# Six pairs' plain products ahead of their products of sums, and the first pair by seven products too

## The chip, the cores and the metric

The kernel runs on one core of a Trainium2 chip. Five engines work side by side, each in its own order: TensorE (PE in the profile, its weight loads PEld) for matrix products, VectorE (DVE), ScalarE (ACT) and GpSimd (POOL) for elementwise work, and SyncE (SP), which issues most loads and stores. The metric is the time on the device in microseconds (us), a median over runs. Before the change it is 539.0 us, the median of three runs from 539.0 to 539.04.

## The reference

A gated feed-forward layer over 2048 tokens, in bf16.

```python
B, S, D, F = 1, 2048, 1024, 3584
def _gelu(x):
    return jax.nn.gelu(x, approximate=True)
def reference(x, w_gate, w_up, w_down):
    return (_gelu(x @ w_gate) * (x @ w_up)) @ w_down
```

## The kernel before

**Tiles and halves.** The tokens go in two halves (`h` 0 and 1) of 1024; a half has two blocks of 512 (`tb` 0 and 1). The 3584 columns of gate and up are 28 tiles of 128, two neighbouring tiles make a pair, and a chunk (`chunks[(h, c)]`) is four tiles: 1 MB of gate and 1 MB of up. D = 1024 is eight slices of 128, `kd` 0 to 7; the upper half of the rows is `kd` 0 to 3, the lower half 4 to 7. One matmul takes a 128x128 piece of weights and a 128x512 piece of the transposed x, which is kept as `xT[0]` and `xT[1]`, and adds into one of eight PSUM banks. The banks are used in twos, one for gate (`j` = 0) and one for up (`j` = 1): PB, VB, QB, RB.

**Seven products instead of eight.** For a pair, the two tiles, the two halves of the rows and the two token blocks make a 2x2 by 2x2 block product. `quads` (L406) does it with seven block products of four matmuls, for gate and for up, so 56 matmuls where the plain way takes 64. M1 and M2 (L441 to L452) are plain: the upper and the lower rows of the pair's first tile with `xT[0]`. M5, M6, M7, M3 and M4 are products of sums: `s1` to `s4` and a copy `a22` are made from the weights by `s_sum` (L367), `t1` to `t4` and a copy `b22` from x by `t_sum` (L241). The sums of weights have one buffer each, so those for the next pair (`prep`, L460) are made behind the product that read the old ones: by GpSimd at L388, `a22` by ScalarE at L401. The sums of x are made once in a half, by VectorE at L262 and ScalarE at L251; they are then kept.

In a pair ScalarE copies M1 into Q (L444), M5 into SBUF (L472) and M6 into R (L478), VectorE adds M5 (L434) to Q and to both V, ScalarE applies gelu (L286), and VectorE multiplies gate by up into h (`hT`, L291). M7 and M4 add into R; up's M4 needs the bank from which VectorE has just added M5 into V. Engines that are handed instructions run them in the order in which the code emits them; the helpers `pe`, `dve`, `act`, `pool` and `sp` (L119 to L140) fix that.

**The start.** `first_pair_units` (L329) does pair 0 the plain way: 32 matmuls with `xT[0]` and 32 with `xT[1]` (`part`, L323, `mm_gu`, L265), while the sums of x and those of pair 1 are made. Its first x block is loaded as it lies and transposed on TensorE for `kd` 0 to 3 (`transpose_x0`), the rest comes by transposing DMA (`load_xT`). Loads of the first tiles stand on SyncE's and ScalarE's queues by hand (L187 to L233). Then `quads` runs pair 1 alone, with `thens` entry `early`: the next pair's `s1` and `s2` are made late, a piece of `t4` goes to GpSimd, and `pool_behind_dve` (L136) makes GpSimd wait for VectorE at one place. From pair 2 on `quads` takes two pairs at a time: both M1 and M2, then both pairs' products of sums.

**Work beside it.** In the first half of the tokens VectorE also makes sums of the down weights (`stage_step`, L625), which SyncE stores to DRAM (`t_dram`) for later; there are 42 such steps and four of `s_down`, run a few at a time by `run_steps`. After the 14 pairs `down_group` does h times the down weights, also by seven products, and then the second half follows.

Of the kernel before, what the change touches and what calls it, by code (L numbers as in the profile page):

```python
# [11 lines left out]
F32 = mybir.dt.float32  # L12
# [22 lines left out]
def kernel(  # L35
# [106 lines left out]

    xs0 = w_mem[:, 4 * CH : 4 * CH + TSB * D].rearrange("p (a b) -> p a b", b=D)
    chunks = {}

    def new_chunk(key):
        c0 = 2 * CH * (key[1] % 2)
        chunks[key] = tuple(
            w_mem[:, c0 + j * CH : c0 + (j + 1) * CH].rearrange(
                "p (a b) -> p a b", b=FG  # L150
            )
            for j in range(2)
        )
# [33 lines left out]
    load_x0(0, sp, 0, 2)  # L187
    load_x0(0, act, 2, TSB)
    load_w(first, 0, 0, 2, sp, 0, FA)
    load_x0(1, act)  # L190
    load_w(first, 1, 0, 2, sp, 0, FA)
    load_w(first, 0, 2, 5, act, 0, FA)
    load_w(first, 1, 2, 5, sp, 0, FA)
# [20 lines left out]
    load_xT(xT, 0, 0, KH, KH + 1)  # L214
    behind_transpose = last_on["sp"]
    load_xT(xT, 0, 0, KH + 1, KH + 2)
    for j in range(2):
        load_w(first, j, 5, KD, act, 0, FA)
        tc.add_manual_dep(
            last_on["act"].ins,  # L220
            behind_transpose.ins.name,
            SCHED_DEP,
            reason="engine order",
        )
    act(nc.scalar.preload_act_table(ACT.Gelu_apprx_tanh))
    load_xT(xT, 0, 0, KH + 2, KD)
    for k0, k1 in ((0, 2), (2, KH), (KH, KD)):
        load_xT(xT, 0, 1, k0, k1)
    for j in range(2):
        load_w(first, j, 0, KD, sp, FA, FG)  # L230
    new_chunk((0, 1))
    for j in range(2):
        load_w((0, 1), j, 0, KD)  # L233
# [31 lines left out]
    def mm_gu(ps, w_sb, fi, tb, kd):  # L265
        pe(
            nc.tensor.matmul(  # L267
                ps[:],
                lhsT=w_sb[:, kd, fi * P : (fi + 1) * P],
                rhs=xT[tb][:, kd, :],  # L270
                start=(kd == 0),
                stop=(kd == KD - 1),
            )
        )

# [23 lines left out]
    def unit_out(hT, bset, fi, tb):  # L299
        mult(hT, gelu(banks[bset[0]]), banks[bset[1]], fi, tb)  # L300

    def transpose_x0(q):

        parts = [(2 * q, 0, 4), (2 * q + 1, 0, 4)]
        if q == 0:
            parts = [(0, 0, 2), (0, 2, 4), (1, 0, 4)]
        for n, (kd, ts0, ts1) in enumerate(parts):
            tp = banks[(PB + QB)[(2 * q + n) % 4]][:].bitcast(BF16)
# [14 lines left out]
    def part(held, tb, k0, k1, us=(0, 1), js=(0, 1)):  # L323
        for kd in range(k0, k1):
            for j in js:
                for u in us:
                    mm_gu(banks[held[u][j]], chunks[first][j], u, tb, kd)

    def first_pair_units(hT):  # L329

        held = (VB, RB)
        transpose_x0(0)
        warm(RB[1], TB // 2)
        part(held, 0, 0, KPQ, js=(0,))
        transpose_x0(1)
        part(held, 0, 0, KPQ, js=(1,))
        part(held, 0, KPQ, KD)
        t_sum("t1", 0, KH // 2)
        t_sum("t1", KH // 2, KH)
        for u in range(2):  # L340
            unit_out(hT, held[u], u, 0)
        held = (QB, PB)
        part(held, 1, 0, KH)
        t_sum("t2")
        t_sum("b22")
        t_sum("t3", 0, KH // 2)
        part(held, 1, KH, KD, (0,))
        unit_out(hT, held[0], 0, 1)
        t_sum("t3", KH // 2, KH)
        part(held, 1, KH, KD, (1,))  # L350
        unit_out(hT, held[1], 1, 1)
        for j in range(2):
            s_sum(0, 1, j, "s3", True, False)
        for name in ("s1", "s2", "s4"):
            for j in range(2):
                s_sum(0, 1, j, name)
# [5 lines left out]
    def block(key, j, i, kh):  # L362
        fi = 2 * (key[2] % PPG) + i
        w_sb = chunks[(key[0], key[2] // PPG)][j]
        return w_sb[:, half(kh), fi * P : (fi + 1) * P]
# [40 lines left out]
    def quads(hT, h, members, nxt, thens, m5_first):  # L406

        last = nxt is None
        run = []
        for n, pair in enumerate(members):  # L410
            after = (h, members[n + 1]) if n + 1 < len(members) else nxt
            first_ = (PB, RB)[n] if len(members) > 1 else VB
            run.append((pair, after, thens[n], first_, (QB, VB)[n]))
# [27 lines left out]
        for pair, _, _, first_, q_ in run:  # L441
# [4 lines left out]
        for pair, _, _, first_, _ in run:  # L446
# [8 lines left out]
        for n, (pair, after, then, _, Q_) in enumerate(run):  # L455
            f0 = 2 * pair
            ends = after is None
            eager = "early" in then

            def prep(j, name, after=after):  # L460
                if after is not None:
                    s_sum(after[0], after[1], j, name)
# [6 lines left out]
            def do_m5(j):  # L469
# [3 lines left out]
                if not eager:  # L473
                    prep(j, "s1")
# [6 lines left out]
            if eager:  # L481
# [9 lines left out]
            for j in range(2):  # L491
                add_m5(Q_[j], Q_[j], m5[j])
                if not eager:
                    prep(j, "s2")
            done(n, "m5")
            for j in range(2):
# [4 lines left out]
                if j == 0 and eager:  # L501
                    pool_behind_dve()
                    for name in ("s1", "s2"):
                        for i in range(2):
                            prep(i, name)
# [3 lines left out]
                else:  # L509
                    mult(hT, g, banks[V_[1]], f0 + 1, 1)  # L510
# [9 lines left out]
            for j in range(2):  # L520
# [4 lines left out]
                else:  # L525
                    mult(hT, g, banks[R_[1]], f0 + 1, 0)
# [541 lines left out]
```

## Time and profile before

| what | value |
|---|---|
| median of the runs | 539.0 us |
| the profiled execution, first to last instruction | 537.4 us |
| matmuls (with transposes and warming ones) | 2388 |
| TensorE busy | 533.6 us, 99% |
| VectorE / ScalarE / GpSimd busy | 68% / 49% / 47% |
| chain, pair 0 (L267) | from 4.98 us to 19.82 us, with transposes between |
| chain, pairs 1 to 13 of the first half (L418) | 163.21 us from 19.82 us |
| chain, first half's down product (L698) | 87.89 us from 183.03 us |
| chain, second half's pairs (L418) | 175.56 us from 270.92 us |
| chain, second half's down product (L698) | 87.95 us from 446.48 us |

The profile shows one execution, so its durations add up to its own 537.4 us; the 1.6 us between that and the median lie outside the first and the last instruction. In a line of the timeline the columns are: start (us from the span's start), length (us), engine, line of the kernel, operation, what is written and read, shapes, and how many instructions are merged; a bracket tells how long the engine was idle before it and what ended that.

### The profile page before, as it was taken

Reading aid. Unit: us, or ns where it says so; the run is one execution under the profiler, and the core shown is the slowest. Engines: PE = TensorE matmul, PEld = TensorE weight load, DVE = VectorE, ACT = ScalarE, POOL = GpSimd, SP = SyncE. Lnnn points to the kernel's source line nnn. Section 1 sums busy time; section 2 is a strip of 40 time slices with the busy share of each in tenths; the row PEclk is TensorE's granted clock in tenths of the full one; section 3 lists DMA queues with packets and bytes.
Section 4 is the critical chain, followed back from the end, with each engine's and each line's share of the span. In section 5 each row is a group of like instructions: output and inputs, shape, how many; then the busy total and the mean of one; then the engine's idle time right before and its main releaser. Section 6 shows DMA issues by size and latency. Waiting matters only on the chain.

```text
span 537.4 us, 7033 instructions
## 1 busy us (share of the span) xinstructions
PE 533.6 (99%) x2388; PEld 379.2 (71%) x2388; DVE 367.6 (68%) x476; ACT 263.5 (49%) x447; POOL 252.2 (47%) x213
## 2 busy tenths in 40 slices
PE   9999999999999999999999999999999999999997
PEld 4568686867677686777768676776768686866866
DVE  2985868787876998989555353444444669979961
ACT  2555555556465329117465554656555551452280
POOL 0698696969696200000056494958677670000000
PEclk9999999999999999999999999999999999999999
DMA  9965759697623887788950413314040329677846
GB/s 220 329 199 134 267 164 304 182 320 199 229 53 143 318 288 243 243 292 292 329 168 12 145 62 97 110 48 154 3 156 22 136 84 337 228 237 250 292 143 212
DMA packets 92547, 102.70 MB, mean 191 GB/s; under 512 B 18656, under 2 KB 67424, under 8 KB 92512
## 3 DMA queue, kind: packets, MB, share of 16 engines
q1 hardware_dynamic: 69568, 80.23, 45.7%
q10 hardware_dynamic: 22944, 22.02, 13.2%
q8 instruction: 19, 0.31, 0.3%
q14 instruction: 16, 0.13, 0.1%
HBM read 85.98 MB, written 12.58 MB: 183 GB/s over the span
## 4 chain that ended last, share of the span: by engine, by line
PE 99%; ACT 0%; issue 0%
PE bank L418 63%; PE bank L698 33%; PE bank L267 3%; PE bank L202 1%; PE bank L311 0%; ACT o_sb L754 0%
## 5 line engine op out<-in xcount | busy, mean ns | idle before, releaser
L418 PE MATMUL bank<-t_mem,s_mem 128*128 128x512 f32 x1056 | 244.6, 392 | 0.0
L418 PEld LDWEIGHTS bank<-t_mem,s_mem 128*128 128x128 f32 x1056 | 198.1, 188 | 42.7 <-issue 0.2
L388 POOL TENSOR_TENSOR s_mem<-w_mem 128x512 fp32r<-128x512 bf16 x102 | 124.0, 1236 | 185.5 <-DMA out_dram<-o_sb 96.9
L698 PE MATMUL bank<-t_mem,s_mem 128*128 128x512 f32 (+1 forms) x548 | 127.2, 391 | 0.0
L698 PEld LDWEIGHTS bank<-t_mem,s_mem 128*128 128x128 f32 x548 | 102.5, 188 | 22.0
L291 DVE TENSOR_TENSOR hT<-w_mem,bank 128x512 bf16<-128x512 f32 x106 | 72.5, 687 | 66.5 <-PE bank L418 44.5
L434 DVE TENSOR_TENSOR bank<-bank,m 128x512 f32<-128x512 f32 x108 | 70.0, 694 | 56.1 <-ACT m L472 54.3
L418 PE MATMUL bank<-xT,w_mem 128*128 128x512 bf16 x432 | 95.7, 379 | 0.0
L286 ACT ACTIVATE w_mem<-bank 128x512 f32<-128x512 f32 x106 | 63.0, 597 | 64.1 <-DVE bank L434 34.8
L418 PEld LDWEIGHTS <-w_mem 128*128 128x128 bf16 x432 | 41.2, 98 | 51.3 <-issue 3.4
L388 POOL TENSOR_TENSOR s_mem<-w_mem,s_mem 128x512 fp32r<-128x512 bf16 x52 | 68.4, 1335 | 2.9 <-PE bank L418 2.9
L600 DVE TENSOR_TENSOR t_mem<-w_mem 128x1024 fp32r<-128x1024 bf16 x56 | 65.9, 1225 | 0.9 <-PE bank L418 0.9
L388 POOL TENSOR_TENSOR s_mem<-s_mem,w_mem 128x512 fp32r<-128x512 f32 x52 | 61.3, 1200 | 0.0
L401 ACT CAST s_mem<-w_mem 128x512 fp32r<-128x512 bf16 x54 | 33.2, 616 | 31.3 <-PE bank L418 30.1
L478 ACT COPY bank<-bank 128x512 f32<-128x512 f32 x54 | 30.8, 570 | 26.6 <-PE bank L418 26.6
L670 DVE TENSOR_TENSOR s_mem<-hT 128x512 fp32r<-128x512 bf16 x52 | 36.7, 745 | 7.1 <-PE bank L698 7.1
L472 ACT COPY m<-bank 128x512 f32<-128x512 f32 x54 | 31.8, 589 | 18.4 <-PE bank L418 18.4
L698 PEld LDWEIGHTS <-hT 128*128 128x128 bf16 x224 | 21.3, 98 | 26.6 <-issue 2.1
L444 ACT COPY bank<-bank 128x512 f32<-128x512 f32 x54 | 30.7, 570 | 14.3 <-PE bank L418 13.5
L625 DVE TENSOR_TENSOR o_sb<-wd_sb,o_sb 128x512 fp32r<-128x512 bf16 x28 | 32.9, 1176 | 0.5
L763 ACT CAST o_sb<-bank 128x512 bf16<-128x512 f32 x27 | 14.8, 585 | 33.8 <-PE bank L698 33.8
L597 ACT CAST t_mem<-w_mem 128x1024 fp32r<-128x1024 bf16 x28 | 26.9, 1047 | 0.0
(46 smaller groups left out, 236.5 us busy)
## 6 DMA issues: line engine op xcount, KB each, us to landing
t_mem<-t_dram SPq DMA_DIRECT2D x56, 512.0 KB, 5.3
w_mem<-in_w_gate_dram ACTq DMA_DIRECT2D x10, 1024.0 KB, 5.4
w_mem<-in_w_up_dram ACTq DMA_DIRECT2D x10, 1024.0 KB, 8.3
wd_sb<-in_w_down_dram SPq DMA_DIRECT2D x28, 256.0 KB, 5.4
t_dram<-o_sb SPq DMA_DIRECT2D x28, 256.0 KB, 3.5
wd_sb<-in_w_down_dram SPq DMA_DIRECT2D x12, 512.0 KB, 7.6
w_mem<-in_w_down_dram SPq DMA_DIRECT2D x4, 1024.0 KB, 6.7
w_mem<-in_w_down_dram SPq DMA_DIRECT2D x8, 512.0 KB, 8.3
```

Source lines behind the costliest of these rows:

```text
L286: act(nc.scalar.activation(out=g_sb, in_=ps[:], func=ACT.Gelu_apprx_tanh))
L291: nc.vector.tensor_tensor(out=hT[:, fc, tb * TB : (tb + 1) * TB], in0=g_sb, in1=ps[:], op=ALU.mult,)
L388: pool(nc.gpsimd.tensor_tensor(out=t, in0=in0, in1=in1, op=op))
L401: act(nc.scalar.copy(out=t, in_=a(1, 1)))
L418: nc.tensor.matmul(banks[bank][:], lhsT=lhs[:, c, :], rhs=rhs[:, c, :], start=start and c == 0, stop=c == KH - 1, skip_group_check=True,)
L434: nc.vector.tensor_tensor(out=banks[dst][:], in0=banks[src][:], in1=m5[:], op=ALU.add)
L472: act(nc.scalar.copy(out=m5[j][:], in_=banks[V_[j]][:]))
L478: act(nc.scalar.copy(out=banks[R_[j]][:], in_=banks[Q_[j]][:]))
L600: dve(nc.vector.tensor_tensor(out=t, in0=in0, in1=in1, op=ALU.subtract))
L625: dve(nc.vector.tensor_tensor(out=t, in0=in0, in1=in1, op=ALU.subtract))
L670: dve(nc.vector.tensor_tensor(out=t, in0=in0, in1=in1, op=op))
L698: nc.tensor.matmul(banks[bank][:, c0:c1], lhsT=lhs(i, u), rhs=rhs(i)[:, c0:c1], start=start and i == 0, stop=stop and i == NS - 1, skip_gr ...
```

## The change

For the first half of the tokens, pairs 0 to 5 are formed anew: pair 0 is tiles 4 and 6, pair 1 tiles 5 and 7, pairs 2 to 5 tiles 0 to 3 with 8 to 11 (`LEAD`). Their first tiles, 0 to 5, are done the plain way with `xT[0]` at the very start, two by two (`PLAIN`): the upper rows of tiles 0 to 3, then their lower rows, then tiles 4 and 5. After the upper rows a bank holds exactly M1 of a pair; ScalarE copies it into a part of h's memory that isn't written yet (`hold`), and the lower rows add M2 on top, which gives that tile's first output. Then `quads` runs the six pairs with `plain=False`: no M1 and M2, M1 is fetched back into Q by ScalarE (`fetch`), and only the products of sums are left. So pair 0 too is done by seven products, and there is no `early` order and no `pool_behind_dve` any more; the order of a pair with `plain=False` is M5, M5, M6, M6, and gate's `s3` of the next pair is made by VectorE, the other sums by GpSimd. Chunks (0,1) and (0,3) lie in h's memory. From pair 6 on all is as before, but the staging steps are shared out anew: two in each of pairs 1 to 5, nine in each later two pairs.

The loads at the start are also set anew: gate weights on SyncE, up weights on ScalarE, all four tiles of chunk (0,0) early, then the second x block, chunk (0,1) in halves, and chunk (0,2).

```diff
+    LEAD = ((4, 6), (5, 7), (0, 8), (1, 9), (2, 10), (3, 11))
+    PLAIN = ((0, 1), (2, 3), (4, 5))
+    HF = 16
+    HELD = ((0, 1), (0, 3))
...
+    def p_hold(pair, j):
+        f = ((8, 9), (10, 11), (12, 13), (14, 15), (24, 25), (26, 27))[pair][j]
+        return hT0[:, f : f + 1, :].rearrange("p a b -> p (a b)").bitcast(F32)
...
+    for j, queue in enumerate((sp, act)):
+        ts = slice(j * TSB // 2, (j + 1) * TSB // 2)
+        load_x0(0, queue, ts.start, ts.stop)
+        load_w(first, j, 0, KPQ, queue, 0, FA)
+        load_x0(1, queue, ts.start, ts.stop)
+        load_w(first, j, 0, KPQ, queue, FA, FG)
+        load_w(first, j, KPQ, KH, queue)
...
+    load_xT(xT, 0, 0, KH, KD)
     for j in range(2):
+        load_w(first, j, KH, KD)
+    for k0, k1 in ((0, KH), (KH, KD)):
         load_xT(xT, 0, 1, k0, k1)
+    new_chunk((0, 1))
+    for k0, k1 in ((0, KH), (KH, KD)):
+        for j in range(2):
+            load_w((0, 1), j, k0, k1)
+    new_chunk((0, 2))
     for j in range(2):
+        load_w((0, 2), j, 0, KD)
...
+    def hold(held, tiles, j):
+        for u, t in enumerate(tiles):
+            pair = [top for top, _ in LEAD].index(t)
+            act(nc.scalar.copy(out=p_hold(pair, j), in_=banks[held[u][j]][:]))
...
+        sets = ((VB, RB), (QB, PB), (VB, RB))
+        def top(n, j, k0, k1):
+            plain_products(sets[n], PLAIN[n], j, k0, k1)
+            if k1 == KH:
+                hold(sets[n], PLAIN[n], j)
+        def rest(n):
+            plain_products(sets[n], PLAIN[n], 0, KH, KD)
+            gelus(sets[n], PLAIN[n])
+            plain_products(sets[n], PLAIN[n], 1, KH, KD)
         transpose_x0(0)
         warm(RB[1], TB // 2)
+        top(0, 0, 0, KPQ)
+        top(0, 1, 0, KPQ)
         transpose_x0(1)
+        top(1, 0, 0, KPQ)
+        top(0, 0, KPQ, KH)
+        top(0, 1, KPQ, KH)
+        top(1, 1, 0, KPQ)
+        top(1, 0, KPQ, KH)
+        top(1, 1, KPQ, KH)
+        rest(0)
+        outs(sets[0], PLAIN[0])
         t_sum("t1", 0, KH // 2)
         t_sum("t1", KH // 2, KH)
+        rest(1)
+        outs(sets[1], PLAIN[1])
         t_sum("t2")
+        t_sum("t3", 0, KH // 2)
+        t_sum("t3", KH // 2, KH)
+        top(2, 0, 0, KH)
+        top(2, 1, 0, KH)
         t_sum("b22")
+        rest(2)
+        outs(sets[2], PLAIN[2])
+        for name in ("s3", "s1", "s2", "s4"):
             for j in range(2):
+                s_sum(0, 0, j, name)
...
+        def fetch(n):
+            for j in range(2):
+                act(nc.scalar.copy(out=banks[run[n][4][j]][:], in_=p_hold(n, j)))
...
             def prep(j, name, after=after):
                 if after is not None:
-                    s_sum(after[0], after[1], j, name)
+                    dve_too = not plain and (name, j) == ("s3", 0)
+                    s_sum(after[0], after[1], j, name, dve_too, False)
...
-            if eager:
+            if not plain:
                 order = (do_m5, 0), (do_m5, 1), (do_m6, 0), (do_m6, 1)
...
                 add_m5(V_[j], R_[j], m5[j])
                 if j == 0:
                     done(n, "v of gate")
-                if j == 0 and eager:
-                    pool_behind_dve()
-                    for name in ("s1", "s2"):
-                        for i in range(2):
-                            prep(i, name)
                 prep(j, "s3")
...
+            thens = [{} for _ in LEAD]
+            thens[0]["start"] = [
+                lambda j=j: s_sum(0, 0, j, "a22") for j in range(2)
+            ] + [lambda: t_sum("t4", 0, KH // 2)]
+            thens[0]["m5"] = [lambda: t_sum("t4", KH // 2, KH - 1)]
+            thens[0]["v of gate"] = [lambda: t_sum("t4", KH - 1, KH)]
+            for n in range(1, len(LEAD)):
+                thens[n]["start"] = [lambda: run_steps(1), run_loads]
+                thens[n]["m3"] = [lambda: run_steps(1), run_loads]
...
+            quads(hT, h, range(len(LEAD)), (h, begin), thens, True, False)
...
-                few = lead == begin
-                add(0, "m1", lambda n=3 if few else 4: run_steps(n))
-                add(0, "start", lambda n=1 if few else 3: run_steps(n))
+                add(0, "m1", lambda: run_steps(4))
+                add(0, "start", lambda: run_steps(3))
```

## The prediction

> **What bounds the kernel now.** I read the busy line and the chain first, then TensorE's timeline over the first 60 us, then GpSimd's and VectorE's over the same stretch, then the load rates.
>
> ```profile
> PE 533.6 (99%) x2388; PEld 379.2 (71%) x2388; DVE 367.6 (68%) x476; ACT 263.5 (49%) x447; POOL 252.2 (47%) x213
> ...
> PE 99%; ACT 0%; issue 0%
> ...
> 6.71 13.11 PE L267 MATMUL bank<-xT,w_mem 128*128 128x512 bf16 x60
> 19.66 3.63 PE L418 MATMUL bank<-xT,w_mem 128*128 128x512 bf16 x16
> 22.93 9.52 PE L418 MATMUL bank<-t_mem,s_mem 128*128 128x512 f32 x40
> 32.29 7.08 PE L418 MATMUL bank<-xT,w_mem 128*128 128x512 bf16 x32
> 39.02 18.51 PE L418 MATMUL bank<-t_mem,s_mem 128*128 128x512 f32 x80
> 57.37 2.98 PE L418 MATMUL bank<-xT,w_mem 128*128 128x512 bf16 x13
> ```
>
> The chain is 99% TensorE and each piece begins where the one before ends, so every matmul taken away is a gain and every new wait of TensorE is a loss, one for one. Prices, start to start: a plain product (19.66 - 6.71) / 60 = 0.216 us, a product of sums (57.37 - 39.02) / 80 = 0.229 us, two pairs by seven products 57.37 - 32.29 = 25.08, so 12.54 a pair.
>
> ```profile
> 15.24 2.29 DVE L262 TENSOR_TENSOR t_mem<-xT,t_mem 128x2048 fp32r<-128x2048 bf16 x1
> ...
> 17.32 1.22 POOL L388 TENSOR_TENSOR s_mem<-w_mem 128x512 fp32r<-128x512 bf16 x1 [16.01 <-DMA w_mem<-in_w_gate_dram]
> 17.45 2.18 DVE L262 TENSOR_TENSOR t_mem<-xT 128x1024 fp32r<-128x1024 bf16 x1
> ...
> 20.14 1.58 DVE L262 TENSOR_TENSOR t_mem<-xT 128x1024 fp32r<-128x1024 bf16 x1
> 20.60 3.72 POOL L388 TENSOR_TENSOR s_mem<-s_mem,w_mem 128x512 fp32r<-128x512 f32 x2
> ...
> 44.45 2.31 POOL L388 TENSOR_TENSOR s_mem<-s_mem,w_mem 128x512 fp32r<-128x512 f32 x2
> 46.71 2.74 POOL L388 TENSOR_TENSOR s_mem<-w_mem 128x512 fp32r<-128x512 bf16 x2
> 47.36 1.07 DVE L625 TENSOR_TENSOR o_sb<-wd_sb,o_sb 128x512 fp32r<-128x512 bf16 x1
> ...
> 62.51 0.68 DVE L625 TENSOR_TENSOR o_sb<-wd_sb 128x512 fp32r<-128x512 bf16 x1
> ```
>
> GpSimd's sums and VectorE's sums of two SBUF operands do not run side by side. Two GpSimd sums alone take 2.31 us; with one 512-wide VectorE sum in them 2.74, and that sum takes 1.07 to 1.53 instead of 0.68. The 1024-wide sum at 17.45 begins with a GpSimd sum under way and lasts 2.18. They take turns: a GpSimd sum holds the place for 1.13 (its cadence), a VectorE sum pushes GpSimd back by 2.74 - 2.31 = 0.43 when 512 wide; a 1024-wide one by 0.97 (3.72 - 2 x 1.13 = 1.46, less 0.43 for the 512-wide one also in it). For 2048 wide I take 2.29 - 0.25 = 2.04, the 0.25 being what the narrower ones leave free. VectorE's work on PSUM (L291, L434: 0.64 apart back to back) doesn't compete.
>
> ```profile
> GB/s 0 154 307 315 180 268 278 256 229 196 324 307 322 354 349 354 374 389 261 37 3 0 71 345 372 351 362 402 315 56 11 0 52 216 91 1 0 91 371 368
> ```
>
> This is the rate in slices of 1.5 us over 0 to 60 us.
>
> **The change part by part.** *Fewer matmuls.* Pair 0 goes from 64 plain products (64 x 0.216 = 13.8) to one seven-product pair (12.54): -1.27 us. Nothing else leaves the path; it is the whole gain.
>
> *TensorE's new order, if nothing made it wait.* The first matmul at 4.93 as before, four at the cold pace, four more, eight transposes: 7.57. The other 88 plain products: 7.57 + 88 x 0.216 = 26.56. Marks on the way: the last two tiles' upper rows begin at 19.65, and pair 0's sums run from 26.56 to 26.56 + 40 x 0.229 = 35.74.
>
> *Loads.* Ahead of chunk (0,1) stand both x blocks and chunk (0,0), 4.19 MB; its four halves of 0.52 MB follow. Summing the slices above, 4.22 MB have moved at 18.0 us, 4.70 at 19.5, 5.24 at 21.0, 5.77 at 22.5, 6.32 at 24.0. So the halves land at about 19.6, 21.0, 22.5 and 24.0, against TensorE's 19.65, 21.4, 23.1 and 24.8: just in time, 0 us. Bounds: 18.0 (fewer 512 B packets) and 21.5 (a second stretch of transposes), so 0 to 1.9.
>
> *Pair 0's operands: the step that decides.* Before, six weight sums were ahead on GpSimd, two `s3` on VectorE, and L262's last piece was put on GpSimd behind VectorE by hand (`pool_behind_dve`). Now GpSimd makes all eight of pair 0's, `s3` first though it is wanted last, and at once pair 1's, while VectorE makes `t2`, `t3` and three pieces of `t4`. VectorE is free for `t2` only at 21.15: two multiplications at 16.2, two pieces of `t1` (1.22 each) to 19.93, two multiplications of tiles 2 and 3. Taking turns from 19.8 (end of `t1`):
> s3 20.93; s3 22.1; t2 24.15; s1 25.3; t3 26.25; s1 27.4; t3 28.35; s2 29.5; s2 30.6; t4 31.6 (VectorE multiplies tiles 4 and 5 between t3 and t4).
> M5 of gate starts at 26.56, M5 of up waits for its s1 (27.5), M6 of gate for its s2 (29.55), M6 of up until 30.7 to 31.6, where without waits it ends at 26.56 + 16 x 0.229 = 30.2: +1.4 us.
> Then s4 32.7; s4 33.85. VectorE adds M5 twice (to 33.1), then stands in line with a 512-wide piece of `t4` (34.3), adds M5 to gate's V (35.1), stands again with the last piece of `t4` (behind pair 1's s1: 35.85), and again with pair 1's gate `s3` (behind the other s1: 37.4), and only then adds M5 to up's V: 38.2. Up's M4, four matmuls into that bank, waits for it: 38.2 to 39.15. TensorE would have ended the pair at 35.74, so +3.4 us, the 1.4 included. As one sum: ten GpSimd turns 11.3, VectorE's turns 2.04 + 3 x 0.97 + 3 x 0.43 = 6.2, 19.8 + 17.6 = 37.4, and the add and M4 behind.
> Bounds: if all three narrow VectorE sums find the place free, 33.1 + 3 x 0.68 + 2 x 0.64 = 36.4, M4 ends at 37.3, +1.6; each that has to wait adds 0.6. Upward 4.8, if the weights land 1.4 us late, so that `t2` goes ahead of both `s3` and everything moves. I take 3.4, since GpSimd's next sums have all they wait for and leave no gap.
>
> The Trainium skill (SBUF — State Buffer, section SBUF: two separate sides) says that a VectorE instruction with two SBUF inputs and a GpSimd one exclude each other for the whole instruction. By whole durations the line would be 10 x 1.17 + 2.29 + 3 x 1.22 + 3 x 0.68 = 19.7 instead of 17.6, and the time 543.3, an estimate by that rule; the trace shows 0.43 and not 0.68 for the narrow sum, so I keep the row.
>
> *Pairs 1 to 5*, 9.18 us each without plain products between. GpSimd: 7 x 1.13 + 3 x 0.43 (gate's `s3` and two staging sums on VectorE) = 9.2. VectorE: 7 x 0.64 + 3 x 1.3 = 8.4. After the delay of pair 0, GpSimd is some 2.5 us ahead of need, which covers 5 x 0.02: 0 us; without that lead up to 1. ScalarE's fetch of M1 is not in the trace; by L478 (570 ns) and L401 (616 ns) 1.2 a pair, and its pair comes to 6.6 of 9.18: 0. Copies into h's memory cost L472's 589 ns each beside matmuls: 0.
>
> *Later.* Staging sums move from pairs 1 to 5 into the last two pairs (nine instead of four steps there). At 168.27 VectorE had waited 2.3 us, which takes three sums, and the first down weights leave SP's queue, behind those sums' stores, at about 167.6 instead of 158.76, landing by 176 against a first use at 175.36: 0, at most 0.5.
>
> *Sum against the execution's own time.* Span 537.4 - 1.27 + 3.4 = 539.5. The runs' 539.0 is 1.6 above the span; with that, 541.2.
>
> **Rivals.** *(1) The floor, faster.* If GpSimd's sums are ready when wanted, nothing is late: 539.0 - 1.27 = 537.7. For it: TensorE hid the same contention before, with one wait of 0.2 us at 26.7. Against it: the eighth port turn (`s2` of gate, 29.5) is already past M6's 28.4, even with weights on time. It decides if s2 of up is ready by 29.3 and up's V is added by 34.8.
> *(2) Little more than the first wait.* The narrow sums find gaps, because GpSimd itself waits for TensorE: +1.6, so 539.0 - 1.27 + 1.6 = 539.3. For it: at 30 us before, GpSimd paused 0.7 us for TensorE. Against it: all it needs for pair 1's `s1` is M5 of pair 0, done at 28.4.
> *(3) Weights late.* The gate half of chunk (0,1) comes after 21 and TensorE waits at once, then `t2` goes first: 539.0 - 1.27 + 4.8 = 542.5. For it: the 1 MB loads of this chunk took 10 and 11 us to land before.
>
> **How the numbers follow.** Forecast 55%, (1) 11%, (2) 16%, (3) 18%. 0.2%, what a measurement of this kernel can tell from no change, is 1.08 us: 537.92 to 540.08. The forecast's own bounds are 539.9 (+2.2, one narrow sum waiting) to 542.5 (+4.8). Faster 0.10: nearly all of (1). Same 0.20: (2) and the low edge of the forecast. Slower 0.70: the rest of it and (3). The range takes in (2), down to 539.1, and a little over (3), to 542.8, and leaves out the floor.
>
> **What would show it.** Right: TensorE's plain products end near 26.6; then its first waits, for `s_mem` from GpSimd inside pair 0's M5 and M6 (1 to 2 us), and before the last four matmuls of that pair a wait for VectorE's add (about 2 us); pair 1 starts near 39; 9.2 us a pair from there with no waits; the rest as before, some 2 us later. GpSimd's sums between 20 and 40 us would take 1.6 and more where VectorE has one in between. Wrong: pair 1 starting before 37 (rival 1 or 2), TensorE waiting for a weight load at 19 to 21 (rival 3), or waits in pairs 2 to 5, where I have none.

## The result, and the profile after

The changed kernel takes 545.86 us (median of four runs, 544.74 to 548.17) where the kernel before takes 539.0 (538.65 to 539.04): 1.0131 times as long, 95% interval 1.0107 to 1.0155. It is slower, as forecast, but by 6.9 us and not by 2.2. The profiled execution took 545.35 us, its span 543.1 against 537.4.

Two lines of the profile's page after, as shown of before, and TensorE's timeline from the last two plain tiles to the end of pair 0 (columns as above):

```profile
PE 533.9 (98%) x2380; PEld 380.9 (70%) x2380; DVE 370.1 (68%) x485; ACT 272.4 (50%) x467; POOL 259.6 (48%) x216
...
PE 92%; SPq 2%; POOL 2%; DMA 2%; DVE 1%; ACT 0%; issue 0%; ACTq 0%
```

```profile
22.08 7.08 PE L329 MATMUL bank<-xT,hT 128*128 128x512 bf16 x32 [2.27 <-DMA hT<-in_w_gate_dram]
28.81 3.08 PE L460 MATMUL bank<-t_mem,s_mem 128*128 128x512 f32 x12
32.80 6.03 PE L460 MATMUL bank<-t_mem,s_mem 128*128 128x512 f32 x24 [0.90 <-POOL s_mem L428]
40.50 47.50 PE L460 MATMUL bank<-t_mem,s_mem 128*128 128x512 f32 x204 [1.68 <-DVE bank L476]
```

The chain is no longer 99% TensorE: 8% of it runs over other engines and loads, nearly all ahead of the last line. There are three waits: 2.27 us for the gate half of chunk (0,1) ahead of tiles 4 and 5, 0.90 for GpSimd's `s2` inside M6 (1.24 against the nominal pace, since the piece before it is stretched too), and 1.68 for VectorE's add to up's V ahead of the last four matmuls of pair 0. These four take 4 x 0.229, so pair 1 begins at 41.42; the forecast said 39.15, the pace without waits 35.74.

VectorE's and GpSimd's timelines over the same stretch:

```profile
20.91 2.29 DVE L274 TENSOR_TENSOR t_mem<-xT,t_mem 128x2048 fp32r<-128x2048 bf16 x1
23.11 4.27 DVE L274 TENSOR_TENSOR t_mem<-xT 128x1024 fp32r<-128x1024 bf16 x2
...
30.41 1.32 DVE L274 TENSOR_TENSOR t_mem<-xT,t_mem 128x1024 fp32r<-128x1024 bf16 x1
33.22 0.70 DVE L476 TENSOR_TENSOR bank<-bank,m 128x512 f32<-128x512 f32 x1 [1.50 <-ACT bank L521]
34.63 0.70 DVE L476 TENSOR_TENSOR bank<-bank,m 128x512 f32<-128x512 f32 x1 [0.71 <-ACT bank L521]
35.24 1.45 DVE L274 TENSOR_TENSOR t_mem<-xT,t_mem 128x512 fp32r<-128x512 bf16 x1
36.61 0.69 DVE L476 TENSOR_TENSOR bank<-bank,m 128x512 f32<-128x512 f32 x1
37.21 1.06 DVE L274 TENSOR_TENSOR t_mem<-xT,t_mem 128x512 fp32r<-128x512 bf16 x1
38.19 1.65 DVE L426 TENSOR_TENSOR s_mem<-hT 128x512 fp32r<-128x512 bf16 x1
39.76 0.69 DVE L476 TENSOR_TENSOR bank<-bank,m 128x512 f32<-128x512 f32 x1
```

```profile
22.11 7.40 POOL L428 TENSOR_TENSOR s_mem<-hT 128x512 fp32r<-128x512 bf16 x4 [20.81 <-DMA hT<-in_w_gate_dram]
29.47 3.27 POOL L428 TENSOR_TENSOR s_mem<-s_mem,hT 128x512 fp32r<-128x512 f32 x2
32.71 2.30 POOL L428 TENSOR_TENSOR s_mem<-hT,s_mem 128x512 fp32r<-128x512 bf16 x2
```

The pattern is the one forecast: `t2` (20.91), `t3`, the first half of `t4` on VectorE between GpSimd's eight sums, two of which alone take 2.3 us and four 7.40 with VectorE's in between; then the adds of M5 (L476) with three narrow sums standing between them, the last at 38.19, each 1.06 to 1.65 us long instead of 0.68. All of it is some 2 us later than forecast.

As a sum over the span's +5.7: 1.27 less for the matmuls saved; pair 1 begins 41.42 - 35.74 = 5.68 late; pairs 1 to 5 take 87.84 - 40.50 = 47.34 us where 204 matmuls at 0.229 make 46.7, +0.6; the first down product takes 88.47 from matmul to matmul, 88.05 before, +0.4; some 0.3 is spread. In this execution 2.25 us lie outside its first and last instruction. Before it is 1.8: each of the 47 executions of the kernel before beside the experiments takes 1.74 to 1.85 us more than its own span. The 1.6 given for it above sets the median of the runs against the span of another execution.

One execution among the experiments, the profiled one of plain_c0 (679.5 us), had TensorE's clock at 0.75 from 5.5 us on; only its loads are read below, and that kernel was run again as plain_c0b.

### The profile page after: what moved, and what is told of

Same layout as the page of the kernel before. It is cut to its first block, busy times and chain, and to the rows that moved or that the text cites. A ratio compares the mean times of both kernels' runs of the same rounds, so it can differ in the third digit from the quotient of the medians.

```text
span 543.1 us, 7102 instructions
## 1 busy us (share of the span) xinstructions
PE 533.9 (98%) x2380; PEld 380.9 (70%) x2380; DVE 370.1 (68%) x485; ACT 272.4 (50%) x467; POOL 259.6 (48%) x216
## 4 chain that ended last, share of the span: by engine, by line
PE 92%; SPq 2%; POOL 2%; DMA 2%; DVE 1%; ACT 0%; issue 0%; ACTq 0%
PE bank L460 60%; PE bank L737 32%; POOL s_mem L428 2%; SPq L190 2%; DMA hT<-in_w_gate_dram 1%; DMA w_mem<-in_w_up_dram 1%; DVE t_mem L274 0%; DVE bank L476 0%; DVE s_mem L426 0%; ACT bank L521 0%; SPq L179 0%; ACTq L185 0%; ACT o_sb L793 0%; ACTq L521 0%
## 5 line engine op out<-in xcount | busy, mean ns | idle before, releaser
L460 PE MATMUL bank<-t_mem,s_mem 128*128 128x512 f32 x1096 | 254.4, 392 | 2.7 <-DVE bank L476 1.7
L460 PEld LDWEIGHTS bank<-t_mem,s_mem 128*128 128x128 f32 x1096 | 204.8, 188 | 49.1 <-DVE bank L476 2.0
L428 POOL TENSOR_TENSOR s_mem<-w_mem 128x512 fp32r<-128x512 bf16 x88 | 104.4, 1207 | 155.6 <-DVE t_mem L274 96.3
L737 PEld LDWEIGHTS bank<-t_mem,s_mem 128*128 128x128 f32 x548 | 102.4, 188 | 22.5 <-issue 0.5
L476 DVE TENSOR_TENSOR bank<-bank,m 128x512 f32<-128x512 f32 x112 | 73.2, 694 | 57.7 <-ACT m L516 44.5
L287 ACT ACTIVATE w_mem<-bank 128x512 f32<-128x512 f32 x106 | 62.9, 597 | 60.7 <-DVE bank L476 36.9
L460 PE MATMUL bank<-xT,w_mem 128*128 128x512 bf16 x320 | 70.8, 380 | 0.0
L428 POOL TENSOR_TENSOR s_mem<-w_mem,s_mem 128x512 fp32r<-128x512 bf16 x46 | 61.6, 1361 | 3.4 <-PE bank L460 3.4
L460 PEld LDWEIGHTS <-w_mem 128*128 128x128 bf16 x320 | 30.5, 98 | 38.0 <-issue 2.6
L428 POOL TENSOR_TENSOR s_mem<-s_mem,w_mem 128x512 fp32r<-128x512 f32 x46 | 54.7, 1208 | 0.0
L521 ACT COPY bank<-bank 128x512 f32<-128x512 f32 x56 | 31.9, 571 | 25.7 <-PE bank L460 25.4
L441 ACT CAST s_mem<-w_mem 128x512 fp32r<-128x512 bf16 x48 | 29.6, 616 | 26.8 <-PE bank L460 25.6
L428 POOL TENSOR_TENSOR s_mem<-hT 128x512 fp32r<-128x512 bf16 x14 | 19.8, 1432 | 27.7 <-DMA hT<-in_w_gate_dram 20.8
L486 ACT COPY bank<-bank 128x512 f32<-128x512 f32 x44 | 25.1, 570 | 11.5 <-PE bank L460 10.8
```

The costliest lines, as they stand in the source:

```text
L287: act(nc.scalar.activation(out=g_sb, in_=ps[:], func=ACT.Gelu_apprx_tanh))
L428: pool(nc.gpsimd.tensor_tensor(out=t, in0=in0, in1=in1, op=op))
L441: act(nc.scalar.copy(out=t, in_=a(1, 1)))
L460: nc.tensor.matmul(banks[bank][:], lhsT=lhs[:, c, :], rhs=rhs[:, c, :], start=start and c == 0, stop=c == KH - 1, skip_group_check=True,)
L476: nc.vector.tensor_tensor(out=banks[dst][:], in0=banks[src][:], in1=m5[:], op=ALU.add)
L521: act(nc.scalar.copy(out=banks[R_[j]][:], in_=banks[Q_[j]][:]))
```

## The experiments

What the theories meant by turns: a sum of two SBUF operands on VectorE and one on GpSimd take turns at a shared place. All runs in one table. Pair 0's begin and end are read from TensorE's timeline. Where its first sum is late (after2, v1_free, plain_c0b), it begins when TensorE is through with the plain products. The end is the start of the long run that follows, plus 0.229 for each matmul of it that still belongs to pair 0; the matmul records have it some 0.1 later. In c1_first, v1_free and s3v a stretch at half clock or a short wait lies in those matmuls, so there the end is the start of pair 1's first matmul. The ratios are to the kernel before on the same chip. On the chip of after2, fetch_early and s3v_fetch that kernel took 541.07 us (538.50 to 542.53) and on the others 539.02 to 539.34, so those three are compared by their ratios.

| run | pair 0 begins | ends | takes | median us | ratio, 95% interval |
|---|---|---|---|---|---|
| the change | 28.81 | 41.42 | 12.6 | 545.86 | 1.0131 (1.0107 to 1.0155) |
| after2 | 27.54 | 41.25 | 13.7 | 545.65 | 1.0089 (1.0056 to 1.0122) |
| no_t34 | 28.13 | 38.06 | 9.9 | 542.67 | 1.0061 (1.0043 to 1.0079) |
| c1_first | 26.08 | 44.15 | 18.1 | 548.09 | 1.0188 (1.0148 to 1.0227) |
| s3_last | 28.61 | 40.00 | 11.4 | 543.21 | 1.0073 (1.0058 to 1.0088) |
| v1_free | 28.52 | 42.07 | 13.5 | 544.15 | 1.0094 (1.0078 to 1.0110) |
| plain_c0b | 27.08 | 42.11 | 15.0 | 545.67 | 1.0124 (1.0098 to 1.0150) |
| sums_c0 | 30.55 | 41.58 | 11.0 | 543.04 | 1.0069 (1.0051 to 1.0086) |
| floor | 26.68 | 37.72 | 11.0 | 541.38 | 1.0037 (1.0021 to 1.0053) |
| act_c1 | 28.81 | 41.43 | 12.6 | 544.98 | 1.0102 (1.0061 to 1.0143) |
| s3v | 29.67 | 40.26 | 10.6 | 543.02 | 1.0068 (1.0053 to 1.0083) |
| tidy | 29.75 | 39.77 | 10.0 | 542.90 | 1.0063 (1.0047 to 1.0080) |
| floor_tidy | 27.34 | 38.49 | 11.2 | 541.08 | 1.0033 (1.0020 to 1.0046) |
| fetch_early | 30.79 | 42.55 | 11.8 | 546.65 | 1.0116 (1.0080 to 1.0152) |
| s3v_fetch | 28.80 | 39.29 | 10.5 | 543.89 | 1.0065 (1.0042 to 1.0088) |

**First question: is it the turns, and which of them?**

no_t34:

```diff
+        if name in ("t3", "t4"):
+            tsum[name] = tsum["t2"]
+            return
```

> Leaves out x's sums t3 and t4: their products take t2 in their place. Turns (my theory: pair 0's waits of 3.45 us are VectorE's sums and GpSimd's pushing each other back): five VectorE sums fewer, 3 x 0.97 + 2 x 0.43 = 3.8 us of turns, more than the wait; so pair 0 runs in 9.2 to 9.6 us instead of 12.6, span about 539.8, time about 542. The wait of 2.3 us at the last two plain tiles stays. Rival (GpSimd's eight sums are too long by themselves for the time they have, or the fetch of M1 sets the pace): the waits inside pair 0 stay at 2 us or more, time 544.5 to 546.

Pair 0 takes 9.9 us and no wait for GpSimd or VectorE is left in it, only 0.4 for ScalarE. VectorE's sums cause both waits; 0.3 to 0.7 us more than expected stay.

s3_last:

```diff
-        for name in ("s3", "s1", "s2", "s4"):
+        for name in ("s1", "s2", "s3", "s4"):
```

> Pair 0's sums on GpSimd in the order of their use: s1, s2, s3, s4. Turns: the number of turns is the same, but s2 comes two GpSimd turns earlier, so TensorE's first wait inside pair 0 (1.24 us) goes; VectorE's adds and its three narrow sums between them then come 1.2 to 2.3 us earlier, and pair 0 takes 10.3 to 11.4 us instead of 12.6: time 543.6 to 544.6. Rival (the length of the whole line alone counts, not its order): the first wait goes and the second grows by the same amount, pair 0 still 12.6, time about 545.8.

11.4 us and 543.21: the order counts. The wait for `s2` is gone and the one for the add is 0.63 instead of 1.68; 0.48 ahead of the first M7, for ScalarE's copies of M6, and 0.29 for GpSimd's `s4` have come instead.

v1_free:

```diff
         rest(2)
+        t_sum("t4", 0, KH // 2)
+        t_sum("t4", KH // 2, KH)
         outs(sets[2], PLAIN[2])
...
-                    dve_too = not plain and (name, j) == ("s3", 0)
+                    dve_too = not plain and n > 0 and (name, j) == ("s3", 0)
...
-            thens[0]["m5"] = [lambda: t_sum("t4", KH // 2, KH - 1)]
-            thens[0]["v of gate"] = [lambda: t_sum("t4", KH - 1, KH)]
```

> t4 is made in one stretch after t3, ahead of the multiplications of tiles 4 and 5, and pair 1's gate s3 goes to GpSimd, so that no narrow VectorE sum stands between the adds of M5. Turns: the wait of 1.7 us for the add to up's V goes, since VectorE comes to it at once; the wait for s2 stays or grows by up to 0.9 (one turn more ahead of it): pair 0 10.9 to 11.8 us, time 544.1 to 545. Rival (up's V is late for GpSimd's or TensorE's sake, and not for the three narrow sums ahead of it on VectorE): the last four matmuls of the pair wait as long as before, time 545.5 to 546.5.

As the turns have it: nothing waits for VectorE's add any more, and the waits for GpSimd's sums grow to 0.88 and 0.90. In the profiled execution the pair takes 13.5 us, since TensorE ran at half clock from 33.4 to 36.9 us (last section); without the 1.7 us that this costs by my estimate, it would be 11.8, the upper edge of what was expected.

s3v (on top of s3_last):

```diff
-                prep(j, "s3")
+                if plain or n > 0:
+                    prep(j, "s3")
+                elif j == 1:
+                    prep(0, "s3")
+                    prep(1, "s3")
```

> s3_last, and pair 1's s3 of gate is made on VectorE after the add to up's V in pair 0, not ahead of it. Order on VectorE (theory): that sum took 1.65 us ahead of the add, so the add comes 1.5 us earlier and the wait of 0.63 us for it goes: pair 0 10.7 to 10.9 us instead of 11.4, time 542.5 to 542.7. Rival (the last matmuls of the pair wait for GpSimd's s4 or ScalarE anyway): 11.3 us and 543.2 as with s3_last.

TensorE's and VectorE's timelines of this run:

```profile
29.67 4.03 PE L460 MATMUL bank<-t_mem,s_mem 128*128 128x512 f32 x16
34.15 52.52 PE L460 MATMUL bank<-t_mem,s_mem 128*128 128x512 f32 x224 [0.45 <-issue]
```

```profile
38.48 0.69 DVE L476 TENSOR_TENSOR bank<-bank,m 128x512 f32<-128x512 f32 x1
39.08 1.05 DVE L426 TENSOR_TENSOR s_mem<-hT 128x512 fp32r<-128x512 bf16 x1
```

The `s3` now stands behind the last add, which ends at 39.17. The timeline merges the 224 matmuls into one line, but by their own records the last four of pair 0 still wait for that add, 0.22 us instead of the 0.63 of s3_last. Pair 0 takes 10.6 us, about as expected. The median is within the noise of s3_last's, though: in the two profiles pair 0 began 1.1 us later here, by chunk (0,1), which landed at 22.9 instead of 21.8. That the load took back the gain in all four runs is not shown.

**Second question: do the late weights and the turns add up?** That was my first reading of the 5.7 us: 2.25 at the loads and 3.45 inside pair 0.

plain_c0 and plain_c0b (the same kernel twice):

```diff
-                w_sb = chunks[(0, t // FPG)][j]
+                w_sb = chunks[(0, 0 if t < 8 else t // FPG)][j]
```

> Tiles 4 to 7 take chunk (0,0)'s columns in the plain products alone (other weights, same work); the sums of pairs 0 and 1 still read chunk (0,1). One line (theory now: what ends pair 0 is the line of GpSimd's and VectorE's turns, which starts when chunk (0,1) lands; TensorE's own wait at 22 lies beside it): the plain products end near 26.6 instead of 28.8, and pair 0 gives all of it back, 14 to 15 us long, pair 1 still begins at 41 to 41.5, span 543 or more (waits closer together can also cost clock). Rival (two losses that add up, 2.25 for the late weights and 3.45 inside the pair): pair 0 stays at 12.6 us, pair 1 begins at 39.2, span 540.8.

> The kernel of plain_c0 once more (tiles 4 to 7 take chunk (0,0)'s columns in the plain products alone), for a profile at full clock. One line: plain products end near 26.6, GpSimd's sums of pair 0 still run without a gap from about 22 to 35, pair 1 begins at 41 to 41.5, span about 543. Rival (two losses that add up): pair 1 begins at 39.2, span 540.8.

The other three spans of plain_c0 were 542.7, 543.0 and 544.0; plain_c0b's profile:

```profile
29.16 2.34 PE L460 MATMUL bank<-t_mem,s_mem 128*128 128x512 f32 x8 [1.73 <-POOL s_mem L428]
32.38 7.14 PE L460 MATMUL bank<-t_mem,s_mem 128*128 128x512 f32 x28 [0.88 <-POOL s_mem L428]
41.19 47.59 PE L460 MATMUL bank<-t_mem,s_mem 128*128 128x512 f32 x204 [1.67 <-DVE bank L476]
```

They don't add up. The wait at the loads is gone, TensorE is through with the plain products at 27.1 us, and it gives the gain back in pair 0, which now takes 15.0. Pair 1 begins at 42.11, 0.6 later than expected, as `t2` began 0.7 later than in the change. TensorE's wait for the load stood beside the real line and cost nothing. after2 and its neighbours say what that line is:

> The changed kernel itself, as a control beside the next two. Both theories: gate half of chunk (0,1) lands 21.4 to 22.9, some 1.2 us after its 512th packet, with the 16 KB code packet at 17.7 to 19.3; pair 0 starts near 28.5 to 29.5 and takes 12.3 to 12.9 us; time 545 to 546.5.

The load landed 1.3 us earlier than in the first profile (20.76 against 22.04), pair 0 could begin 1.3 us earlier, and pair 1 began only 0.17 earlier. VectorE's and GpSimd's lines of after2:

```profile
20.76 2.28 DVE L274 TENSOR_TENSOR t_mem<-xT,t_mem 128x2048 fp32r<-128x2048 bf16 x1
```

```profile
32.56 2.29 POOL L428 TENSOR_TENSOR s_mem<-hT,s_mem 128x512 fp32r<-128x512 bf16 x2
```

What stays the same from run to run is the stretch from the start of `t2` to the end of the second `s4` (here 32.56 + 2.29 = 34.85):

| run | `t2` starts | gate half lands | second `s4` ends | stretch |
|---|---|---|---|---|
| the change | 20.91 | 22.04 | 35.01 | 14.10 |
| after2 | 20.76 | 20.76 | 34.85 | 14.09 |
| plain_c0b | 21.61 | 21.73 | 35.72 | 14.11 |
| fetch_early | 22.05 | 22.33 | 36.16 | 14.11 |
| v1_free, one 1024-wide sum more in it | 21.32 | 21.74 | 36.37 | 15.05 |
| no_t34, three fewer | 21.09 | 21.36 | 32.24 | 11.15 |

The line begins with `t2`, wherever in the first 1.1 us of it the weights land, and one 1024-wide sum on VectorE is worth 0.95 to 0.98 us of it.

sums_c0 is the mirror image:

```diff
-        w_sb = chunks[(key[0], t // FPG)][j]
+        c = t // FPG
+        w_sb = chunks[(key[0], 0 if (key[0], c) == (0, 1) else c)][j]
```

> The mirror image: the sums of pairs 0 and 1 read chunk (0,0)'s columns, the plain products their own chunk (0,1). One line: GpSimd can start near 14 us, when that chunk is there, so all eight sums are made before TensorE wants them; TensorE still waits 1.4 to 2.3 us at the last plain tiles, then pair 0 runs in 9.2 to 9.7 us: pair 1 begins near 38.2, span 539.8 to 540.4. Rival (what delays pair 0 is VectorE's own row of work, the fetch of M1 or the adds, whatever GpSimd does): pair 0 keeps 2 us or more of its waits, span 542 or more.

In between: GpSimd's sums are early and the wait for them is gone, but pair 0 still takes 11.0 us, with 0.44 us of waiting for ScalarE and 0.83 for VectorE's add. The rival has 1.9 of the 2 us it asked for; VectorE's and ScalarE's own rows cost that. In the profiled run half the clock comes on top (last section).

floor (both edits):

> Both together: nothing in the first 40 us reads chunk (0,1). By the one line and the wait at the load: no wait left, pair 0 from 26.6 to 36.2, span 537.6 to 538.3, which is the -1.27 us of the matmuls saved with half a us more for the six pairs in a row. Rival (something else of the change costs: the holding, the fetch, the staging moved to the last pairs): 539 or more.

The rival is right: 541.38. TensorE's timeline of this run from pair 0 on, and ScalarE's:

```profile
26.68 3.99 PE L461 MATMUL bank<-t_mem,s_mem 128*128 128x512 f32 x16
31.11 4.87 PE L461 MATMUL bank<-t_mem,s_mem 128*128 128x512 f32 x20 [0.44 <-ACT bank L522]
36.80 47.48 PE L461 MATMUL bank<-t_mem,s_mem 128*128 128x512 f32 x204 [0.82 <-DVE bank L477]
```

```profile
24.36 2.19 ACT L263 CAST t_mem<-xT 128x512 fp32r<-128x512 bf16 x4
...
27.40 1.13 ACT L456 COPY bank<-hT 128x512 f32<-128x512 f32 x2
28.43 1.17 ACT L442 CAST s_mem<-w_mem 128x512 fp32r<-128x512 bf16 x2
...
30.43 1.11 ACT L522 COPY bank<-bank 128x512 f32<-128x512 f32 x2
```

With nothing late, pair 0 still takes 11.0 us. ScalarE is back to back from `b22` (L263) over the gelus, the fetch of M1 (L456) and `a22` (L442) to the copies of M6 (L522), and the first M7 waits for those; VectorE comes to up's V behind `t4` and `s3` again.

tidy and floor_tidy take both away (s3v, and for ScalarE):

```diff
+        t_sum("b22")
         top(2, 0, 0, KH)
         top(2, 1, 0, KH)
-        t_sum("b22")
...
-            thens[0]["start"] = [
-                lambda j=j: s_sum(0, 0, j, "a22") for j in range(2)
-            ] + [lambda: t_sum("t4", 0, KH // 2)]
+            thens[0]["start"] = [lambda: t_sum("t4", 0, KH // 2)]
+            thens[0]["m6"] = [
+                lambda j=j: s_sum(0, 0, j, "a22") for j in range(2)
+            ]
```

> s3v, and ScalarE's casts of b22 (four, 2.1 us) come before the last two plain tiles' holds instead of ahead of their gelus, its two casts of a22 (1.05 us) after the copies of M6 instead of ahead of M5's. ScalarE as a second row (theory: it is back to back from b22 to the copies of M6, 14 operations of 0.52 us, and the first M7 waits 0.5 us for it): that wait goes, the adds on VectorE come as much earlier: pair 0 9.5 to 10.0 us, time 541.5 to 542.0. Rival (M7 waits because the copy follows M6 directly, however free ScalarE is): the wait stays at 0.4 to 0.5 and the time at s3v's.

> tidy, and nothing of the first 40 us reads chunk (0,1): tiles 4 to 7 take chunk (0,0)'s columns in the plain products and the sums. If the loads, the turns and ScalarE's row are all there is: no wait in pair 0, pair 1 begins near 36.0, and with floor's own 501.7 from there to the end the span is 537.6 to 537.9, so the 1.27 us of matmuls saved only pay for the half a us in pairs 1 to 5 and the rest. Rival (another cost in the start): pair 1 after 36.8, span 538.5 or more.

In tidy the wait for ScalarE is gone, but one of 0.36 for `s4` has come in its place; pair 0 takes 10.0 us instead of s3v's 10.6. The median, 542.90, is s3v's within the noise and misses the 541.5 to 542.0 expected. In floor_tidy the rival is right again, pair 1 at 38.5, and the time, 541.08, is floor's within the noise: GpSimd makes its eight sums from 13.6 to 27.1 us (floor: 8.7 to 22.2), among VectorE's `t1`, `t2` and `t3`, which take 3.54, 3.17 and 3.32 us instead of floor's 3.40, 2.28 and 2.35 and end later for it. Whoever starts first, the two share one line; ScalarE's row stands close behind.

**Third question: can the loads come earlier?**

c1_first:

```diff
-    for k0, k1 in ((0, KH), (KH, KD)):
-        load_xT(xT, 0, 1, k0, k1)
     new_chunk((0, 1))
     for k0, k1 in ((0, KH), (KH, KD)):
         for j in range(2):
             load_w((0, 1), j, k0, k1)
+    for k0, k1 in ((0, KH), (KH, KD)):
+        load_xT(xT, 0, 1, k0, k1)
```

> The four loads of chunk (0,1) go ahead of xT[1]'s two on SP. Weights late (theory: 2.25 us of the loss is only this chunk landing after TensorE wants it): TensorE's plain products run through to 26.6 us without the wait of 2.3, and what xT[1] gives is later by some 6 us, so t1 ends near 26 and t2 near 28.5, and the waits go into pair 0; in all 0 to 2 us better than the change, 544 to 546. Rival (the wait comes from something else, such as TensorE's bank or the two instruction streams): the gap before the last two tiles stays at about 2 us, and the time gets worse than 546 by the later x.

The plain products run through to 26.4, as expected; `t1` ends at 26.5, `t2` at 30.8, two us later than I had put it, and TensorE waits 1.94 us for it. With the clock lost on top (last section) the time is worse than either theory had it.

act_c1:

```diff
-    for k0, k1 in ((0, KH), (KH, KD)):
-        for j in range(2):
-            load_w((0, 1), j, k0, k1)
+    for j in range(2):
+        load_w((0, 1), j, KH, KD)
...
         top(1, 0, 0, KPQ)
+        for j in range(2):
+            load_w((0, 1), j, 0, KH, act)
```

> The two halves of chunk (0,1) that are wanted first are issued on ScalarE near 9 us instead of on SP behind xT[1], so that they move while SP makes the transposing loads. Issue theory (SP's slow transposing issues, with the rate at 105 to 117 KB/us, hold the chunk back and not the bytes): the gate half lands by 18 to 19.5, the wait of 2.3 goes, the line of turns starts 2 us earlier, and pair 1 begins near 39.2: span 540.5 to 541.5, time about 542.8. Rival (the bytes count, or copies and transposing loads shut each other out): what these 1.05 MB gain xT[1] loses, 3 us, t1 and t2 come as much later, and the time stays at 545 to 547.

The rival is right: the gate half lands at 13.8, but xT[1] at 20.6 and 23.9 instead of 16.1 and 20.7, and chunk (0,0)'s rest later too. Issuing that half on another queue didn't help. Whether the bytes count, or copies and transposing loads shut each other out, this run doesn't tell.

The gate half of chunk (0,1) is 512 packets of 1 KB. Counted in the trace's DMA records from the end of the transposing loads on, 512 had moved 1.1 to 2.2 us before it landed. fetch_early and s3v_fetch asked why:

```diff
-    for i in range(NWARM):
+    for i in range(NWARM // 2):
         warm(i)
+    for i in range(16):
+        warm(3 + i % 4, P)
```

> Four of TensorE's seven warming matmuls (512 wide) become 16 of 128 columns, which take the same time but 24 instructions more, so TensorE comes to each stretch of its code some 12 products (2.6 us) earlier. Code packet (theory): it moves to 15 to 16 us, in the middle of xT[1]'s transposing loads; the gate half of chunk (0,1) then lands within 0.3 us of its 512th packet, 20 to 21 instead of 21.4 to 22.9, and as everything in pair 0 hangs on that landing, pair 1 begins 1 to 1.5 us earlier and the time is 544.0 to 544.8. Rival (the landing is late because sixteen DMA engines finish unevenly anyway): landing still over 1 us after the 512th packet, time 545 to 546.5. Third (the packet waits for the transposing loads and not for TensorE's place in the code): it stays at 17.7 to 19.3 whatever TensorE has done.

> s3v with the same warming matmuls. Code packet (theory): another 1.0 to 1.3 us less than s3v's 543.0: 541.7 to 542.0. Rival: 543.0. Under either it stays behind the kernel before.

The packet of code came at 15.6 and 16.0 us, so it follows TensorE's place in its code. The lag fell to 0.58 and 0.66 us: less than the 1 us of the rival and more than the 0.3 of the theory, so the packet is at most a part of the lag (last section). The ratios were no better, 1.0116 against 1.0089 of after2 and 1.0065 against 1.0068 of s3v: little was moved while the packet came, now amid the transposing loads, and in fetch_early the gate half landed at 22.33, after2's at 20.76. The profile of s3v_fetch also has one wait of 1.80 us at 140.9 us, for VectorE's `hT` (L294), which no other profile has; its cause is open.

## Why the prediction was right or wrong

**The sign and the mechanism were right.** "Taking turns" predicted a wait inside M5 and M6 (1.4 forecast, 1.24 measured), one for VectorE's add before the last four matmuls of pair 0 (about 2, measured 1.68), and no waits in the later pairs but small ones. That the sizes agree so well is in part luck: TensorE came to pair 0 2.25 us later than forecast, at 28.81, while the line of turns was late by about as much. Where it came at 27.08 (plain_c0b), it waited 1.73 and 0.88 us for GpSimd. The price of a turn holds: from `t2` to the last `s4` the prices of before give 8 x 1.13 + 2.04 + 3 x 0.97 = 14.0, and 14.1 was measured in four profiles, one turn more or three fewer moving it as priced. The whole-instruction lock that the Trainium skill (SBUF — State Buffer, section SBUF: two separate sides) states would make it 8 x 1.17 + 2.29 + 3 x 1.22 = 15.3; the trace does not agree, and 14.1 decides.

**Where it failed: the step "Taking turns from 19.8 (end of t1)".** It let both `s3` go ahead of `t2`, because the loads were to be "just in time". The gate half landed at 22.04 and not at 19.6, so VectorE's `t2` took the place at 20.91 and the whole line of turns lay 1.16 us later: the last `s4` ended at 35.01 instead of 33.85. The sum of bytes had been right (the 512th packet of the chunk had moved at 19.81); a load's landing is later than that. Rival (3) describes just this, "then `t2` goes first", and priced it at 4.8 us where 5.68 came. That TensorE itself waits 2.27 us there costs nothing of its own, as plain_c0b showed.

**The second failure: the order of the turns near the end of the line.** The sum had "s2 29.5; s2 30.6; t4 31.6": both `s2` ahead of `t4`. In the timeline `t4`'s first half starts at 30.41, just before up's `s2` could at 30.6, so that one ends at 29.47 + 3.27 = 32.74: 1.16 for the late line and 0.97 for a turn that came ahead of it. M6 of up waits for it, and VectorE's two adds of M5 stand behind M6: they were done at 35.33 (33.1 forecast), just after the last `s4` (35.01). So the first narrow piece of `t4` missed the place that the forecast gave it, directly behind that `s4`. Pair 1's first `s1` (34.97) went ahead of it, the next piece came one turn later too, and the narrow `s3` at 38.19 stands behind pair 1's `s2` and not behind its `s1`: eleven GpSimd turns instead of ten, 1.13 us. The line's late start and this turn, 1.16 + 1.13 = 2.29, make the 2.27 us by which pair 1 is late: up's V at 40.45 (38.2 forecast), the pair at 41.42 (39.15).

**Small terms.** "Pairs 1 to 5: 0" was 0.6: read matmul by matmul, each pair's first M7 comes 0.08 us late, pair 1's 0.4, behind ScalarE's copy of M6, which now comes right before it. "Later: 0" was right: the first down product took 88.05 again in after2, and the 0.4 of the first profile was that execution's. The "1.6" between span and time was a median against another execution's span; by its own executions it is 1.8 before and 2.25 here. The change's kernel and six of its variants have 2.2 to 2.3, seven variants 1.8 and two 2.0; what makes the difference stays open. So from 541.2 to 545.86 there are 2.27 for pair 0, 0.6 for pairs 1 to 5, 0.4 for that down product, 0.3 spread, 0.65 for this term, and 0.5 by which the profiled execution lies below the median.

**The rivals.** The floor (1), 537.7, can't be had by timely weights: floor, which needs none of them, takes 541.38, since VectorE's and ScalarE's rows in pair 0 were not free either; ScalarE's "0" was taken from its busy share of a later pair. Rival (2) fell because the narrow sums found no gaps: they took 1.45, 1.06 and 1.65 us instead of 0.68.

The best variants of the change itself, s3v and tidy, take 542.9 to 543.0 us, some 2.9 less than the change; by the matmul records pair 1 begins 1.3 and 1.7 us earlier. They stay 0.6 to 0.7% behind the kernel before (ratios 1.0068 and 1.0063); the change itself had 1.0131 on its chip and 1.0089 on another.

## What to carry to other kernels

When two engines share a place, write down one line of their turns and find who opens it: where that line is the bound, a wait of the main engine beside it is worth nothing, as plain_c0b showed, while the order of the turns alone (s3_last) brought pair 1 forward by 1.4 us. An engine that is half idle over a whole phase can be back to back in the 7 us that decide, so price it there. And a load has landed when its slowest share has, not when the sum of bytes says so.

## What the runs showed of the hardware that was not expected

**TensorE's clock can halve after short waits.** Stretches of c1_first (columns: from:to, length, busy time of PE, PEld, DVE, ACT and POOL, granted clock, share of the DMA engines, GB/s):

```profile
24.00:28.00 4.00, 3.53 (x17) 1.83 (x15) 4.00 (x5) 3.21 (x7) 4.00 (x3) 1.00 1.01 306
28.00:32.00 4.00, 2.06 (x9) 1.40 (x9) 4.00 (x2) 2.98 (x6) 3.38 (x2) 1.00 1.09 364
32.00:36.00 4.00, 3.44 (x9) 1.94 (x7) 4.00 (x4) 0.57 (x1) 3.75 (x2) 0.52 0.72 265
```

After four us in which it was busy for two, the clock was at half for 10.2 us, from 32.2 to 42.4. v1_free shows it after two waits of 0.9 us (half from 33.4 to 36.9), sums_c0 and fetch_early after one of 2.2 and 2.9, where the next 32 plain products took 8.74 and 8.77 us instead of 7.08. Waits of 2.27 (the change), 2.60 (tidy) and 2.09 us (s3v_fetch) brought no drop. In two of the change's four runs the mean clock was 0.997 and the span 544.1 and 545.9 against 542.5 and 543.1, so this is likely part of its spread.

What the drops have in common shows when the time is cut as the clock records cut it: a stretch at half clock inside the program lasts 3.41 us or three times that, and each full stretch is a whole number of such steps too. TensorE's busy share of the step ahead of a drop was 0.16 (fetch_early), 0.37 (sums_c0), 0.43 (c1_first) and 0.48 (v1_free). No step with more than 0.49 was followed by a drop; five with 0.39 to 0.49 were not followed by one either (two in s3v_fetch, one each in s3v, tidy and plain_c0b). The 2.27 us of the change fall into two steps, busy for 0.53 and 0.81. The clock came back behind the first step that was busy throughout (0.99 or 1.00); the two before it in c1_first, 0.83 and 0.82 busy, left it at half. So by these profiles a step less than half busy can cost the clock and need not, and how a wait falls on the steps may decide what it costs. The Trainium skill (TensorE: Matmul & The Clock Gate, section What's actually happening) gives half the clock after an idle window of about 3.4 us; here no idle time was that long, so in these runs a partly idle window was enough, sometimes.

**While one packet of program code came, a load was late, or all of them nearly stopped.** The DMA view of the change from 16 to 20 us, and stretches of fetch_early:

```profile
q8 instruction: 1, 0.02, 3.3%
```

```profile
14.00:16.00 2.00, 2.00 (x11) 0.91 (x10) 0.00 (x0) 1.08 (x2) 0.00 (x0) 1.00 1.98 235
16.00:18.00 2.00, 2.00 (x11) 0.88 (x9) 1.28 (x2) 0.20 (x1) 0.00 (x0) 1.00 0.44 6
```

One 16 KB packet takes 3.3% of sixteen engines' 4 us, 2.1 us of one engine. In the change it came at the end of the transposing loads, and the gate half landed 2.23 us after its 512th packet; with packets of 1.0 to 1.24 us in nine other profiles that lag was 1.1 to 1.4. One profile (tidy) had 1.68 with a packet of 0.96.

The packet is not the whole lag. In the trace the load reports in sixteen shares, one for each DMA engine, and has landed when the last one is written. In ten of the eleven profiles with the packet near that place the last share came 0.31 to 1.21 us behind the fifteenth (1.20 in the change; v1_free has 0.04); in the five with the packet elsewhere it came 0.01 to 0.18 behind. So the packet probably held up one share. The rest looks like sixteen engines that don't finish together, as the rival of fetch_early had it: in the slow profile of plain_c0 the packet came at 23.2 us, after the landing at 21.6, and the lag was still 1.1.

In fetch_early the packet, 1.95 us long, came amid the transposing loads, and for nearly two us almost nothing moved: 6 GB/s, after 235. In s3v_fetch, with 1.10 us at the same place, it was 73 over those two us. That the packet stopped the loads is read from the two falling together; no run here has the packet elsewhere and the loads the same.
